# Windowed attention into a mixture-of-depths layer: half-block probability operands, sums closed one unit later, and stores on another queue

## The chip, the core and the metric

The kernel runs on one core of a Trainium2 chip. A core has a matrix engine (TensorE, PE in the profile; its weight loads are listed as PEld), a vector engine (VectorE, DVE), an engine for activation functions (ScalarE, ACT), a general one (GpSimd, POOL) and SyncE (SP), which here only starts transfers. Each engine works through its own list of instructions in order; semaphores order work between engines. Matmuls write to PSUM, a small accumulator memory; the other data lie in SBUF. DMA engines carry data between the chip's main memory and SBUF; a transfer is started by an instruction on SyncE's or on GpSimd's queue. The metric is the time in microseconds on the device. The hardware profiler records one execution; its span, from the first to the last instruction, is a little shorter than the time.

## The reference

There are 4 batches of 8 heads, 768 positions and head size 64. Attention lets a query see the 128 latest positions up to its own, and the first 4 positions (the sinks). A second stage picks, in each batch, the 128 rows with the largest gate score and adds a gated two-layer network to them.

```
scores = scale * q @ k^T
keep   = (key < 4) | (0 <= query - key < 128)
a      = softmax(where(keep, scores, -1e9))
x      = a @ v                      # heads side by side: (4, 768, 512)
score  = x @ w_gate
top    = the 128 rows of largest score in each batch
out    = x;  out[top] += sigmoid(score[top]) * relu(x[top] @ w1) @ w2
```

## The kernel before

**Tiling.** A batch is cut into six blocks of 128 positions. With keys of block `kc` on the partitions, the queries that see them lie in blocks `kc` and `kc + 1`: 256 columns, or four squares of 64 for each half block of keys. In a square the mask leaves everything, a triangle, or nothing. For the first key half the squares are diagonal triangle, full, opposite triangle, empty; for the second they are empty, diagonal, full, opposite. Heads are handled in two groups `g` of four.

**Scores.** `scores(st, kc, g)` writes two PSUM tiles `sc`, one for each parity of head, by 64 x 64 tiles of the array (L279), adds the masks by matmuls of an identity with mask tiles (L290), and takes exp on ACT into `pt` (L296), which is f32: [128 keys, 4 heads, 256 queries]. Masked squares become zeros.

**Sums.** `pv_sinks(st, j, g)` starts the PSUM tile `xg` of query block `j` with the sink terms (L316, for j >= 2). `pv(st, j, g)` adds the products of probabilities and values (L326) for key blocks `j - 1` and `j`, each with all 128 keys, so that one of its two half blocks of queries meets a square of zeros in each. The values `vbuf` have a column of ones, so that the softmax denominators come out as a 65th column. Then DVE normalizes: L332 takes the reciprocal and L335 multiplies into `x`. `xg` has three PSUM buffers.

**After a block.** `finish_block` stores `x` to `out` (L340, on GpSimd's queue; in batch 0 the stores are held back and issued three at a time in the first two units of batch 1) and, in the last batch, also to `x_last` on SyncE's queue (L346), casts `x` to bf16 on ACT there (L349), and takes the gate scores by a reducing DVE instruction into `junk` and `scol` (L351). `compare` spreads the scores of a block over the partitions by a TensorE transpose (L358) and an ACT copy (L359) and counts larger ones on DVE (L362), for the ranking. `moe_steps` makes the selection of the batch before: a matrix `E`, the row index `idx` (L399) and an indirect gather `xe` from `out` on GpSimd's queue (L406). `mlp_steps` is the two-layer network of batches 0 to 2, run in batch 3 and in the tail; its result is added to `out` by an indirect store (L438). `moe_last` does the same for batch 3 in the tail, with a gather from `x_last` (L504) and a last indirect store (L530).

**Order.** The order on every engine is written out by hand. `unit(b, j, gs)` is one step: sinks of block `j`, scores of block `j + 1`, loads, sums of block `j`, then transposes of the next batch's queries and keys (L251, with copies L255 on DVE and L257 on ACT and four sink columns `ksk` by GpSimd, L259), pieces of the selection and of the network, the comparison of block `j - 1`, and the end of block `j`. Batch 0 takes the head groups one after the other; batches 1 to 3 take both in a unit.

**Loads.** The next batch's values go over SyncE's queue (L92), its keys and queries, cast to bf16 on the way, over GpSimd's (L123), a pair of heads at a time; the network's weights too (L232, L235). A load is made to wait for the latest exp (`exps[-1]`), so that it doesn't run ahead. GpSimd's order in a unit is keys, `ksk`, the gather if there is one, the store of `x`, queries.

Of the kernel before, what the change touches and what calls it, by code (L numbers as in the profile page):

```python
# [9 lines left out]
FP32 = mybir.dt.float32  # L10
BF16 = mybir.dt.bfloat16
# [20 lines left out]
def kernel(  # L32
# [22 lines left out]
    xp = ctx.enter_context(tc.tile_pool(name="xp", bufs=11))  # L55
# [31 lines left out]
    def wait_for(ins, other):  # L87
        tc.add_manual_dep(ins.ins, other.ins.name, mybir.DependencyInfo(
            mybir.DependencyClass.Sync, mybir.DependencyReason.DATA), reason="pace of the loads")
# [12 lines left out]
    def new_state(b):  # L102
        st = BatchState()
        st.b = b
        st.kq, st.pt, st.cm, st.x, st.kf, st.qf, st.xg = {}, {}, {}, {}, {}, {}, {}
        st.v = vbuf[b % 2]
        st.vsk = vsk[b % 2]
        st.ksk = ksk[b % 2]
        return st
# [45 lines left out]
    trif = xp.tile([128, 3, 64], FP32, name="trif", tag="x")  # L155
    nc.vector.memset(trif[:, :, :], 0.0)
    nc.vector.memset(trif[:, 1, :], MASK_NEG)
# [6 lines left out]
    for e in range(2):  # L164
        rows = trif[64 * e:64 * e + 64]
        nc.gpsimd.affine_select(out=rows[:, 2, :], in_=rows[:, 2, :], compare_op=ALU.is_ge,
                                fill=MASK_NEG, base=0, pattern=[[1, 64]], channel_multiplier=-1)
        nc.gpsimd.affine_select(out=rows[:, 0, :], in_=rows[:, 0, :], compare_op=ALU.is_ge,
                                fill=MASK_NEG, base=-1, pattern=[[-1, 64]], channel_multiplier=1)
    msk = cp.tile([128, 2, 3, 64], BF16, name="msk", tag="msk")  # L170
    nc.vector.tensor_copy(out=msk[:, :, :, :], in_=trif[:, :, :].unsqueeze(1).to_broadcast((128, 2, 3, 64)))
    for e in range(2):
        nc.vector.memset(trif[64 * e:64 * e + NSINK, :, :], 0.0)
    msk0 = cp.tile([128, 2, 3, 64], BF16, name="msk0", tag="msk0")
    nc.vector.tensor_copy(out=msk0[:, :, :, :], in_=trif[:, :, :].unsqueeze(1).to_broadcast((128, 2, 3, 64)))
# [90 lines left out]

    exps = []

    def scores(st, kc, g):
        nq = 256 if kc + 1 < NB else 128  # L270
        pt = st.pt[kc, g] = pp.tile([128, 4, 256], FP32, name="pt", tag="pt")
        sc = [ps.tile([128, 2, 256], FP32, name="sc", tag="ps") for _ in range(2)]
        for hh in range(2):
            hp = 2 * g + hh
            for kh in range(2):
                k0 = kc * 128 + 64 * kh
                q0, q1 = (64, nq) if kh else (0, nq if kc == 0 else min(nq, 192))
                for e in range(2):
                    nc.tensor.matmul(  # L279
                        out=sc[e][es[kh], hh, q0:q1], lhsT=st.KT[es[e], hp, k0:k0 + 64],  # L280
                        rhs=st.QT[es[e], hp, kc * 128 + q0:kc * 128 + q1],
                        start=(hh == 0), stop=False, skip_group_check=True)
        sq = [((2, 4), (0, 2)), ((0, 1), (3, 4))] if nq == 256 else [((0, 1), (0, 2))]
        for r, pair in enumerate(sq):
            for kh in range(2):
                s0, s1 = pair[kh]
                m0 = 2 if (s0, s1) == (0, 1) else 1 if s0 == 0 else 0
                m = msk0 if kc == 0 and kh == 0 else msk
                for e in range(2):
                    nc.tensor.matmul(  # L290
                        out=sc[e][es[kh], :, 64 * s0:64 * s1].rearrange("p h (s n) -> p h s n", n=64),
                        lhsT=ident_b[es[e], es[e]], rhs=m[es[e], :, m0:m0 + s1 - s0, :],
                        start=False, stop=(r == len(sq) - 1), skip_group_check=True)
        po = pt[:, :, :].rearrange("p (a e) n -> p e a n", e=2)
        for e in range(2):
            exps.append(nc.scalar.activation(out=po[:, e, :, 0:nq], in_=sc[e][:, :, 0:nq], func=ACT.Exp,  # L296
                                             scale=0.125))
# [11 lines left out]

    def pv_sinks(st, j, gs):  # L310
        for g in gs:
            st.xg[g] = x_ps.tile([128, 4, VS], FP32, name="xg", tag="xg")
        for m in range(2 if j >= 2 else 0):
            q0 = (j - 2) * 128 + 64 * m
            for g in gs:
                nc.tensor.matmul(out=st.xg[g][es[m], :, :], lhsT=st.psk[es[g], q0:q0 + 64],  # L316
                                 rhs=st.vsk[es[g], :, :], start=True, stop=False, skip_group_check=True)

    def pv(st, j, g):
        xg = st.xg[g]  # L320
        terms = [(j, 0)] if j == 0 else [(j - 1, 128), (j, 0)]
        for hh in range(4):
            h = 4 * g + hh
            for kc, off in terms:
                for m in range(2):
                    nc.tensor.matmul(out=xg[es[m], hh, :],  # L326
                                     lhsT=st.pt[kc, g][:, hh, off + 64 * m:off + 64 * m + 64],
                                     rhs=st.v[:, kc, h, :],
                                     start=(j < 2 and hh == 0 and kc == terms[0][0]),
                                     stop=(hh == 3 and kc == j), skip_group_check=True)  # L330
        rz = sp.tile([128, 4, 1], FP32, name="rz", tag="rz")
        nc.vector.reciprocal(out=rz[:, :, :], in_=xg[:, :, D:D + 1])  # L332
        if g == 0:
            st.x[j] = xp.tile([128, DM], FP32, name="x", tag="x")
        nc.vector.tensor_tensor(  # L335
            out=st.x[j][:, 256 * g:256 * g + 256].rearrange("p (h d) -> p h d", h=4),
            in0=xg[:, :, 0:D], in1=rz[:, :, :].to_broadcast((128, 4, D)), op=ALU.mult)

    def store_x(st, j):
        nc.gpsimd.dma_start(out=out[st.b, j * 128:(j + 1) * 128, :], in_=st.x[j][:, :])  # L340

    def finish_block(st, j):
        if st.b:
            store_x(st, j)
        if st.b == B - 1:
            nc.sync.dma_start(out=x_last[j * 128:(j + 1) * 128, :], in_=st.x[j][:, :])  # L346
            if j == 0:
                st.xb = mp.tile([128, NB, DM], BF16, name="xb", tag="xb")
            nc.scalar.copy(out=st.xb[:, j, :], in_=st.x[j][:, :])  # L349
        junk = mp.tile([128, DM], BF16, name="junk", tag="junk")  # L350
        nc.vector.tensor_tensor_reduce(  # L351
            out=junk[:, :], in0=st.x[j][:, :], in1=wgb[:, :], scale=1.0, scalar=0.0,
            op0=ALU.mult, op1=ALU.add, accum_out=st.scol[:, j:j + 1])


    def compare(st, j):
        bc = ps.tile([128, 128], FP32, name="bc", tag="ps")
        nc.tensor.transpose(out=bc[:, :], in_=st.scol[:, j:j + 1].to_broadcast((128, 128)), identity=ident_f[:])  # L358
        nc.scalar.copy(out=st.sbc[:, j * 128:(j + 1) * 128], in_=bc[:, :])  # L359
        n = 128 * (j + 1)  # L360
# [174 lines left out]
    def start_state(st):  # L535
# [12 lines left out]
    qk_loads_0 = {(0, 4): ([(0, 0)], []), (0, 5): ([(0, 1)], []), (1, 0): ([(1, 0)], [(1, 1)]),  # L548
                  (1, 1): ([(2, 0)], [(2, 1)]), (1, 2): ([(3, 0)], [(3, 1)])}
# [4 lines left out]
    def loads(b, j, gs, end):  # L554
        nxt = states.get(b + 1)
        gate = None if end else exps[-1]
# [19 lines left out]

    def unit(b, j, gs):
# [4 lines left out]
        pv_sinks(st, j, gs)  # L582
        if j == 0:
            for g in gs:
                scores(st, 1, g)
                pv(st, 0, g)
            loads(b, j, gs, 0)
            pack_sinks(st, gs)
            sink_scores(st, gs)
        else:  # L590
            if j + 1 < NB:
                for g in gs:
                    scores(st, j + 1, g)
            elif ahead:
                scores(ahead, 0, 0)
            if (b, j) != (B - 1, NB - 1):
                loads(b, j, gs, 0)
            if ahead and j == 5:
                transposes(ahead, 3 if b else 2)
            if b == 0 and gs[0] == 0 and j >= 4:  # L600
                transposes(st, j - 2)
            for g in gs:
                pv(st, j, g)
                if end and g == 0:
                    compare(st, j - 1)
        first = 2 if b else 3
        if ahead and first <= j <= (4 if b else 5):
            transposes(ahead, j - first if j < 5 else 3)
# [4 lines left out]
        if last and not end and (j or b):  # L613
            compare(*((st, j - 1) if j else (states[b - 1], NB - 1)))
        if b and j == 1:
            next(select[b - 1])
        if (b, j) in layers_late:
            next(mlp[layers_late[b, j]], None)
        if last:
            finish_block(st, j)  # L620
        loads(b, j, gs, 1)
        if b == 1 and j < 2:
            for i in range(3 * j, 3 * j + 3):
                store_x(st0, i)
# [65 lines left out]
```

## Time and profile before

| What | Value |
|---|---|
| Time, median of 3 runs | 159.06 us (157.86 to 159.28) |
| Span of the profiled execution | 155.5 us |
| exp, `pt<-sc` 128x512, L296 | 80 times, 616 ns |
| products of probabilities and values, L326 | 1408 records (two for each f32 product), 49.9 us of PE busy |
| sinks, L316 | 128 records, 13.9 us of PE busy |
| scores and masks, L279 and L290 | 384 and 352 records |
| stores of `x`, L340, on GpSimd | 24, 650 ns each, 5.6 us to landing |
| software queue (GpSimd's), hardware queue (SyncE's) | 51.4% and 25.6% of the 16 DMA engines' span |

Busy time counts an engine's own work; a wait is put down to what released it last, and where the named releaser had long been done, the wait was for something else, often a transfer. Pages and timelines give a line as L326, the engine, the operation, what it writes and what it reads (`out<-in`) and its shape; a number in brackets at the end is the idle time of the engine just before, with its releaser. PEclk is the granted TensorE clock in tenths of full speed, and DMA the mean busy share of the 16 DMA engines.

### The profile page before, as it was taken

The numbers are of one execution on the slowest core, as the hardware profiler recorded it, in microseconds if no ns is written. First come the engines' busy times: TensorE is split into PE (matmuls) and PEld (weight loads), VectorE is DVE, ScalarE is ACT, GpSimd is POOL, SyncE is SP. The second block draws the span as 40 slices with busy tenths as digits, with TensorE's granted clock in tenths as the row PEclk, the third lists the DMA queues.
The fourth block names the chain that finished last, engine by engine and source line by source line (L and its number), as shares of the span: only waits on it lengthen the run. The fifth ranks groups of instructions, "written<-read, shape, count | busy, mean of one in ns | idle before, by whom it ended". The sixth has DMA issues, their size and how long they took to land.

```text
span 155.5 us, 6898 instructions
## 1 busy us (share of the span) xinstructions
PE 128.6 (83%) x3014; PEld 99.7 (64%) x3019; DVE 88.6 (57%) x274; ACT 81.4 (52%) x168; POOL 61.9 (40%) x125
## 2 busy tenths in 40 slices
PE   6979998998899696908999897939999999999300
PEld 2446886876768674905968776828698786867000
DVE  6337264679868754431688957557738338572100
ACT  3367537765695472303596575435966773353000
POOL 4275041742329350671217464533530270547020
PEclk9999999999999999675899999999999999999985
DMA  4989357899919999599559999995999447283310
GB/s 164 275 144 163 86 115 117 142 196 205 229 30 205 268 292 275 109 193 201 134 130 193 184 223 170 248 226 124 181 172 233 112 97 245 26 251 46 93 67 0
DMA packets 39424, 25.52 MB, mean 164 GB/s; under 512 B 26465, under 2 KB 36065, under 8 KB 39394
## 3 DMA queue, kind: packets, MB, share of 16 engines
q0 software_dynamic: 12224, 15.60, 51.4%
q1 hardware_dynamic: 27170, 9.47, 25.6%
q8 instruction: 24, 0.39, 1.0%
q14 instruction: 6, 0.05, 0.2%
HBM read 24.15 MB, written 8.91 MB: 213 GB/s over the span
## 4 chain that ended last, share of the span: by engine, by line
DMA 29%; PE 28%; issue 18%; POOL 8%; ACT 7%; DVE 5%; POOLq 1%; ACTq 0%
DMA qb<-in_q_dram 18%; PE xg L326 9%; DMA out_dram<-gye,idx 7%; PE trp L251 5%; ACT pt L296 4%; DMA xe<-out_dram,idx 3%; POOL out_dram L340 3%; PE w L82 3%; PE xg L316 3%; PE sc L279 3%; DVE KT L255 2%; POOL ksk L259 2%; PE sc L290 2%; ACT QT L257 2%; POOL kb L123 1%
## 5 line engine op out<-in xcount | busy, mean ns | idle before, releaser
L296 ACT ACTIVATE pt<-sc 128x512 f32<-128x512 f32 (+1 forms) x96 | 47.0, 579 | 13.6 <-PE sc L290 13.3
L326 PE MATMUL xg<-vbuf,pt 128*64 128x65 f32 x1408 | 49.9, 227 | 1.0 <-ACT pt L296 0.6
L326 PEld LDWEIGHTS xg<-vbuf,pt 128*64 128x64 f32 x1408 | 45.2, 140 | 5.8 <-issue 1.2
L257 ACT COPY QT<-trp 128x768 bf16<-128x768 bf16 x16 | 12.8, 799 | 28.5 <-PE trp L251 28.4
L362 DVE SCALAR_TENSOR_TENSOR cm<-sbc,scol,tie 128x128 bf16<-128x128 f32 (+5 forms) x23 | 15.3, 665 | 15.1 <-ACT sbc L359 15.0
L279 PE MATMUL sc<-QT,KT 64*64 64x192 bf16 (+3 forms) x384 | 21.0, 251 | 2.2 <-issue 0.8
L332 DVE RECIPROCAL rz<-xg 128x4 f32<-128x4 f32 x48 | 8.7, 181 | 23.6 <-PE xg L326 23.5
L335 DVE TENSOR_TENSOR x<-xg,rz 128x256 f32<-128x256 f32 x48 | 20.4, 424 | 1.7
L290 PE MATMUL sc<-msk,ident_b 64*64 64x256 bf16 (+1 forms) x352 | 19.1, 249 | 0.0
L340 POOL DMA_DIRECT2D out_dram<-x x24 | 15.0, 650 | 8.9 <-DVE x L335 6.5
L279 PEld LDWEIGHTS <-KT 64*64 64x64 bf16 x384 | 11.9, 109 | 10.3 <-issue 5.7
L123 POOL DMA_DIRECT2D kb<-in_k_dram x14 | 10.2, 730 | 19.5 <-ACT pt L296 18.9
L255 DVE COPY KT<-trp 128x768 bf16<-128x768 bf16 x16 | 15.2, 951 | 3.4 <-PE trp L251 3.3
L251 PE MATMUL trp<-ident_b,qb 128*64 128x128 bf16 x192 | 9.0, 236 | 9.2 <-DMA qb<-in_q_dram 9.2
L351 DVE CUSTOM_DVE_ANT_0 junk<-x,wgb 128x512 bf16<-128x512 f32 x24 | 16.5, 686 | 0.1
L259 POOL TENSOR_SCALAR_AFFINE_SELECT ksk<-KT 64x4 bf16<-64x4 bf16 x32 | 7.5, 233 | 18.4 <-DVE KT L255 15.8
L316 PE MATMUL xg<-vsk,psk 64*64 64x260 f32 x128 | 13.9, 426 | 0.3 <-DVE rz L332 0.3
L251 PEld LDWEIGHTS <-qb 128*64 128x64 bf16 x192 | 7.0, 121 | 10.0 <-DMA qb<-in_q_dram 10.0
L290 PEld LDWEIGHTS <-ident_b 64*64 64x64 bf16 x352 | 11.7, 110 | 0.0
L251 PE MATMUL trp<-ident_b,kb 128*64 128x128 bf16 x192 | 9.3, 233 | 2.2 <-issue 1.3
L123 POOL DMA_DIRECT2D qb<-in_q_dram x14 | 10.1, 723 | 0.2 <-issue 0.2
L251 PEld LDWEIGHTS <-kb 128*64 128x64 bf16 x192 | 6.7, 117 | 4.9 <-issue 3.1
(113 smaller groups left out, 137.7 us busy)
## 6 DMA issues: line engine op xcount, KB each, us to landing
out_dram<-x POOLq DMA_DIRECT2D x24, 256.0 KB, 5.6
vbuf<-in_v_dram SPq DMA_DIRECT2D x18, 256.0 KB, 6.2
kb<-in_k_dram POOLq DMA_DIRECT2D x14, 192.0 KB, 6.0
qb<-in_q_dram POOLq DMA_DIRECT2D x14, 192.0 KB, 6.2
w_sb<-in_moe_w_dram POOLq DMA_DIRECT2D x8, 256.0 KB, 6.5
vbuf<-in_v_dram SPq DMA_DIRECT2D x12, 128.0 KB, 3.6
x_last<-x SPq DMA_DIRECT2D x6, 256.0 KB, 3.9
kf<-in_k_dram SPq DMA_DIRECT2D x2, 384.0 KB, 4.0
```

What stands on the lines that cost most here:

```text
L123: ins = nc.gpsimd.dma_start(out=ob[:, :, :, :].rearrange(flat), in_=in_)
L251: nc.tensor.transpose(out=trp[es[h], c, :], in_=src[:, h, c, :], identity=ident_b[:])
L255: nc.vector.tensor_copy(out=o, in_=i)
L257: nc.scalar.copy(out=o, in_=i)
L279: nc.tensor.matmul(out=sc[e][es[kh], hh, q0:q1], lhsT=st.KT[es[e], hp, k0:k0 + 64], rhs=st.QT[es[e], hp, kc * 128 + q0:kc * 128 + q1], sta ...
L290: nc.tensor.matmul(out=sc[e][es[kh], :, 64 * s0:64 * s1].rearrange("p h (s n) -> p h s n", n=64), lhsT=ident_b[es[e], es[e]], rhs=m[es[e], ...
L296: exps.append(nc.scalar.activation(out=po[:, e, :, 0:nq], in_=sc[e][:, :, 0:nq], func=ACT.Exp, scale=0.125))
L316: nc.tensor.matmul(out=st.xg[g][es[m], :, :], lhsT=st.psk[es[g], q0:q0 + 64], rhs=st.vsk[es[g], :, :], start=True, stop=False, skip_group_ ...
L326: nc.tensor.matmul(out=xg[es[m], hh, :], lhsT=st.pt[kc, g][:, hh, off + 64 * m:off + 64 * m + 64], rhs=st.v[:, kc, h, :], start=(j < 2 and ...
L335: nc.vector.tensor_tensor(out=st.x[j][:, 256 * g:256 * g + 256].rearrange("p (h d) -> p h d", h=4), in0=xg[:, :, 0:D], in1=rz[:, :, :].to_ ...
L340: nc.gpsimd.dma_start(out=out[st.b, j * 128:(j + 1) * 128, :], in_=st.x[j][:, :])
L351: nc.vector.tensor_tensor_reduce(out=junk[:, :], in0=st.x[j][:, :], in1=wgb[:, :], scale=1.0, scalar=0.0, op0=ALU.mult, op1=ALU.add, accum ...
```

## The change

There are four parts.

1. **Stores.** `x` is stored over SyncE's queue as soon as it is there, in batch 0 as well. GpSimd issues no plain stores any more. The loads of batch 1's keys and queries are spread over eight units from (0, 2) on. A load at the end of a unit now waits for the unit's last product (`late[0]`).
2. **Scores.** For key blocks 2 to 4 the empty squares are dropped from the layout: a head takes 192 columns, and the second key half is shifted by 64, so that 448 columns are written and exponentiated instead of 512. The mask of both triangles of a half is one matmul for each array tile.
3. **Half-block operands.** For query blocks from the third on, `pv` multiplies with all 128 keys only for the two squares where both halves count; `pv_halves` multiplies the other two squares with 64 keys each, on 64 x 64 tiles of the array, ahead of `pv`.
4. **Sums closed a unit later.** The sinks, the normalization and all that follows from it move to the front of the next unit (`close`); of `compare`, the part on PE and ACT becomes `spread`, and the part on DVE is done a unit later. Halves and sinks write one PSUM region from different rows of the array, so `fence` puts a small DVE memset between them. The last unit has an order of its own, with the sinks between the two groups' products and the halves at the end.

The diff, cut to its core:

```diff
     def scores(st, kc, g):
-        nq = 256 if kc + 1 < NB else 128
-        pt = st.pt[kc, g] = pp.tile([128, 4, 256], FP32, name="pt", tag="pt")
+        w, k0 = width(kc), kc * 128
+        pt = st.pt[kc, g] = pp.tile([128, 2, 512], FP32, name="pt", tag="pt")
...
+                if w == 192:
+                    q0, q1 = (64 * hh, 256) if kh else (0, 192 + 64 * hh)
...
+        elif w == 192:
+            marks = [(kh, slice(0, 2), slice(0, 3, 2)) for kh in range(2)]
...
         for e in range(2):
-            exps.append(nc.scalar.activation(out=po[:, e, :, 0:nq], in_=sc[e][:, :, 0:nq], func=ACT.Exp,
-                                             scale=0.125))
+            exps.append(nc.scalar.activation(out=pt[:, e, 0:n], in_=sc[e][:, 0:n], func=ACT.Exp, scale=0.125))
...
+    def fence(st, j, gs, ins, i, n):
+        if i == 0 and (j, gs) in st.fence:
+            wait_for(ins, st.fence[j, gs])
+        elif i == n - 1 and (j, gs) not in st.fence:
+            mark = sp.tile([1, 1], FP32, name="mark", tag="mark")
+            st.fence[j, gs] = nc.vector.memset(mark[:, :], 0.0)
+            wait_for(st.fence[j, gs], ins)
...
+    def pv_halves(st, j, gs):
+        for g in gs:
+            for hh in range(4):
+                for m in range(2):
+                    f = first(st, j, g, m)
+                    ins = nc.tensor.matmul(out=st.xg[j, g][es[m], hh, :],
+                                           lhsT=prob(st, j - m, g, hh, es[m], 3 * m),
+                                           rhs=st.v[es[m], j - m, 4 * g + hh, :], **f)
+                    fence(st, j, gs, ins, 8 * gs.index(g) + 2 * hh + m, 8 * len(gs))
...
     def pv(st, j, g):
-        terms = [(j, 0)] if j == 0 else [(j - 1, 128), (j, 0)]
+        terms = {0: [(0, 0), (0, 1)], 1: [(0, 2), (0, 3), (1, 0), (1, 1)]}.get(j, [(j - 1, 2), (j, 1)])
...
     def finish_block(st, j):
-        if st.b:
-            store_x(st, j)
+        nc.sync.dma_start(out=out[st.b, j * 128:(j + 1) * 128, :], in_=st.x[j][:, :])
...
-    qk_loads_0 = {(0, 4): ([(0, 0)], []), (0, 5): ([(0, 1)], []), (1, 0): ([(1, 0)], [(1, 1)]),
-                  (1, 1): ([(2, 0)], [(2, 1)]), (1, 2): ([(3, 0)], [(3, 1)])}
+    qk_loads_0 = {(i // 6, i % 6): ([((i - 2) // 2, i % 2)], []) for i in range(2, 10)}
...
-        gate = None if end else exps[-1]
+        gate = late[0] if end else exps[-1]
...
+    def close():
+        for st, j, gs in left:
+            pv_sinks(st, j, gs)
+            for g in gs:
+                normalize(st, j, g)
+        for st, j in ranks:
+            compare(st, j)
...
     def unit(b, j, gs):
...
-        pv_sinks(st, j, gs)
+        close()
...
+        elif end:
+            pv(st, j, 0)
+            pv_sinks(st, j, gs)
+            pv(st, j, 1)
+            spread(st, j - 1)
+            compare(st, j - 1)
+            pv_halves(st, j, gs)
+            cast_x(st, j - 1)
+            for g in gs:
+                normalize(st, j, g)
+            cast_x(st, j)
         else:
...
+            if j >= 2:
+                pv_halves(st, j, gs)
+                left.append((st, j, gs))
             for g in gs:
+                if g == gs[-1] and ahead and j == 5:
+                    transposes(ahead, 3)
...
                 pv(st, j, g)
+                if j == 1:
+                    normalize(st, 1, g)
-        first = 2 if b else 3
-        if ahead and first <= j <= (4 if b else 5):
-            transposes(ahead, j - first if j < 5 else 3)
+        if ahead and 2 <= j <= 4:
+            transposes(ahead, j - 2)
...
-        if b == 1 and j < 2:
-            for i in range(3 * j, 3 * j + 3):
-                store_x(st0, i)
```

## The prediction

> **What bounds the kernel now.** First the page's summary, slices and clock: it shows where TensorE is not full.
>
> ```profile
> span 155.5 us, 6898 instructions
> PE 128.6 (83%) x3014; PEld 99.7 (64%) x3019; DVE 88.6 (57%) x274; ACT 81.4 (52%) x168; POOL 61.9 (40%) x125
> PE   6979998998899696908999897939999999999300
> PEclk9999999999999999675899999999999999999985
> DMA  4989357899919999599559999995999447283310
> ```
>
> PE is full in most slices, so it paces the attention. The hole is at slices 16 to 19 (62 to 78 us), where the clock falls too. Next the table by stretch, cut at the batches (columns: PE, PEld, DVE, ACT, POOL busy with instruction counts, clock, DMA share, GB/s): batches 0 to 3, then the stretch after the last sums.
>
> ```profile
> 10.25:41.00 30.75, 29.41 (x740) 22.55 (x739) 19.17 (x57) 19.31 (x39) 11.77 (x29) 1.00 0.91 155
> 41.00:77.20 36.20, 27.99 (x705) 23.11 (x704) 20.58 (x60) 17.46 (x38) 16.35 (x32) 0.86 0.87 190
> 77.20:106.50 29.30, 25.05 (x710) 20.66 (x706) 20.37 (x61) 16.99 (x37) 12.98 (x25) 1.00 0.98 196
> 106.50:131.90 25.40, 25.05 (x602) 20.11 (x604) 16.00 (x55) 17.69 (x40) 8.51 (x11) 1.00 0.72 164
> 135.00:155.50 20.50, 9.90 (x131) 7.15 (x132) 5.61 (x21) 4.16 (x8) 5.77 (x8) 0.87 0.38 91
> ```
>
> PE is idle 8.2 us in batch 1 and 4.2 in batch 2, hardly at all in 0 and 3. The waits and PE's timeline name the reason; of the five waits of L251 for `qb`, the ones in batch 1 are 1.38, 1.03 and 4.64 us (7.05 in all), in batch 2 0.59 and 1.58, besides 0.92 of "issue".
>
> ```profile
> PE trp L251 <- DMA qb<-in_q_dram: 9.2, 5, 4.6
> 65.57 0.50 PE L251 MATMUL trp<-ident_b,kb 128*64 128x128 bf16 x12
> 70.71 0.85 PE L251 MATMUL trp<-ident_b,qb 128*64 128x128 bf16 x12 [4.64 <-DMA qb<-in_q_dram]
> ```
>
> Last, GpSimd's timeline and the landing times of the stores issued in 50 to 57 us say why that `qb` was late.
>
> ```profile
> 54.31 0.54 POOL L340 DMA_DIRECT2D out_dram<-x  x1 [2.22 <-DMA qb<-in_q_dram]
> 55.06 0.54 POOL L340 DMA_DIRECT2D out_dram<-x  x1 [0.21 <-issue]
> 56.10 0.72 POOL L123 DMA_DIRECT2D kb<-in_k_dram  x1 [0.49 <-ACT sbc L359]
> 56.87 0.42 POOL L259 TENSOR_SCALAR_AFFINE_SELECT ksk<-KT 64x4 bf16<-64x4 bf16 x2
> 63.37 1.04 POOL L406 DMA_INDIRECT xe<-out_dram,idx  x1 [6.08 <-DVE scol L351]
> 64.41 0.58 POOL L340 DMA_DIRECT2D out_dram<-x  x1
> 64.98 0.73 POOL L123 DMA_DIRECT2D qb<-in_q_dram  x1
> DMA to landing us min/median/max: 7.4/8.3/9.6
> ```
>
> The gather `xe` of batch 0 reads `out`, so it needs batch 0's stores, six of which are held back into batch 1. The last goes out at 55.06; with the median landing of 8.3 it is there at 63.4, and the gather starts at 63.37. Its index was ready at 55.2 (L399 ran at 55.02), and `scol`, the name given, is nothing the gather reads: it is a DMA wait under another name. Behind it in GpSimd's order stands the `qb` that PE needs: issued 64.98, landed 70.7.
>
> [...]mean clock 0.51 at 61.5 to 65.0 and 0.50 at 70.7 to 75.2. [...]So moved stores leave DMA work nearly as it is; what is saved is order and GpSimd's time.
>
> **The change part by part.**
>
> *Stores to SyncE, none held back.* 24 issues, 15.0 us busy by row L340, leave GpSimd, and with them its waits for `x`. Batch 0's stores now end early in the first unit of batch 1, two units (some 8 us) before its gather, so the 6.08 us block goes. On SyncE the `v` loads queue behind a store; they are for the next batch, with a batch of slack, so this costs nothing. Of the 7.05 us of `qb` waits in batch 1 I leave 1.5, since DMA is busy there (share 0.87): -5.5. The clock: half speed over 3.5 us (61.5 to 65.0) and 4.5 us (70.7 to 75.2), PE full in both, costs (3.5 + 4.5)/2 = 4.0; [...]I take back 3.7. **Batch 1: -9.2.** In batch 2 the `qb` issues no longer follow a store's 0.58 us issue and 256 KB in the same queue, and the last pair's transposes come later in their unit: of 0.59 + 1.58 + 0.92 = 3.09 us I take **-1.8**.
>
> *Scores of blocks 2 to 4.* The diagonal squares are masked in 4 matmuls instead of 8. Per array tile: before 192 + 192 score columns and 256 + 128 mask columns, 768; after 192 + 256 and 256, 704. Eight 192-column matmuls on four tiles take 0.17 us (85.32 to 85.49), two a tile, so 0.43 ns a column. 64 x 0.43 = 27 ns, times 3 blocks x 2 groups x 4 batches = 24: **-0.65**. The exp goes from 512 to 448 columns; rows of 616 ns (512) and 389 ns (256) give 0.89 ns a column, 57 ns each, 48 times: 2.7 us of ACT, beside PE, so nothing on the path.
>
> *Half-block operands.* For blocks 2 to 5 (4 x 2 groups x 4 batches = 32 times) the 16 products of 128 rows become 8 of 128 rows and 8 of 64. The 16 take 1.08 us (16.23 to 17.31, where 32 records are 16 f32 products), so 8 save 0.54. The 8 halves sit on two diagonal tiles, four on each; no row shows such a product. Four sinks of 260 columns on four tiles take 0.49 us (84.83 to 85.32), 1.88 ns a column, 122 ns for 65 columns: 0.49 if the two tiles overlap, 0.98 if not. [...]I take 0.50, since the scores overlap across tiles: -0.04 x 32 = **-1.3** (bounds -2.9 and +14).
>
> *Sums closed a unit later.* The sinks move from the front of their unit to the front of the next, and with them normalization, store, `junk` and comparison. Same instructions, plus one DVE memset a unit: bounded by the shortest row, a 0.15 us DVE instruction, and by 0.3 with its two hand-overs. It stands behind the halves and is needed a unit later, and what queues behind it on DVE are the `KT` copies, which wait for PE work issued after the halves: nothing. With three `xg` buffers the second group's halves wait for the first group's normalization (0.18 + 0.42 us by L332 and L335); scores (0.77, 85.32 to 86.09) and the first group's halves (0.5) cover it: nothing.
>
> *Tail.* In the last unit nothing covers it. Before, from its first sinks (131.88) to the last `junk` (135.91 + 0.69) are 4.7 us. After, from the previous block's sinks: 0.6, two normalizations 1.2, `junk` and comparison 0.8 + 0.8, the mark, the next comparison 1.1, normalizations 1.2, `junk` 0.7, about 6.7 with the hand-overs; 0.6 of that left the unit before. **+1.4** (bounds 0 and 2).
>
> *Batch 0.* Six stores come into it, two of eight k/q loads fewer stand in its second half; DMA share there is 0.91 over the batch. The last `qb` is now issued one unit later and needed in the middle of block 5, about 5 us on against a median landing of 6.2: **+0.7** (0 to 1.5).
>
> Sum: -9.2 - 1.8 - 0.65 - 1.3 + 1.4 + 0.7 = -10.85; 159.06 - 10.85 = **148.2 us**.
>
> **Rivals.**
> *A, DMA takes over.* Batches 1 and 2 hold 36.2 x 0.87 + 29.3 x 0.98 = 60.2 us of DMA time; without batch 0's six stores (0.67 us each: 256 KB at the 42 ns a KB and engine of the `x_last` packets, over 16 engines), 56.2. My forecast gives the two 65.5 - 11 - 1 = 53.5 us, a share of 1.05. Packets overlap, and 1.10 is seen at 65.6 to 70.7, which speaks against; but if 0.98, batch 2's mean, is the most over a whole batch, they take 57.3: +3.8, **152.0**.
> *B, halves do not overlap.* +0.44 instead of -0.04 for each of 32: +14.1 + 1.3 = 15.4, **163.6**, slower than before. For it: no such product is in the trace. Against: scores and sinks overlap on all four tiles.
> *C, the deferred closing makes a new wait.* DVE is 70% busy in batch 2 (20.37 of 29.3). Were PE to wait one normalization (0.6) in each of the 12 late units of batches 1 to 3, it is 7.2: **155.4**. Against: the cover of 1.3 us above.
>
> **How the numbers follow.** Forecast 0.64, A 0.14, C 0.12, B 0.10. Range 145.5 to 156.0: below, halves at 0.45 (-1.6) and tail and batch 0 at no cost (-2.1), not all together; above, A and C. B is left out. Faster by over 1%: forecast, A and half of C, 0.84; C's worse half within 1%, 0.06; B slower, 0.10.
>
> **What would show it.** Right: no long wait of `xe` or of L251 for `qb` in batch 1, the clock full until the tail, batch 1 some 27 us; halves of both groups near 1.0 us; GpSimd without stores; the tail after the last PE products no shorter. Wrong: DMA share near 1 with waits for `qb` in their old places (A), halves near 2 us (B), or PE waiting for L332/L335 at every unit (C).

## The result, and the profile after

The changed kernel takes **149.86 us** (median of 4 runs, 148.54 to 152.28), the kernel before 159.17 us beside it (4 runs, 157.86 to 160.79). The ratio is **0.9413, with a 95% interval of 0.9305 to 0.9522**. The forecast was 148.2 us, 1.7 us too low. (The ratios here leave disturbed, slower executions out, so a ratio need not be the quotient of two medians, and of four kernels below, with the stores at once on GpSimd, held back on SyncE, with fewer loads and with the old last unit, the profile shows such a slower execution.)

The page's summary and slices of the changed kernel, the same lines that were shown of the kernel before:

```profile
span 147.9 us, 6752 instructions
PE 126.7 (86%) x2923; PEld 99.2 (67%) x2923; DVE 89.3 (60%) x294; ACT 78.5 (53%) x168; POOL 47.2 (32%) x103
PE   6879999999899959989997796979995999999800
PEclk9999999999999996999999999999999999999995
DMA  4839799599996999899469999997996364390801
```

The hole of four slices is gone; dents are left, the deepest (the two 5s) at 52 to 55 and at 111 to 115 us, and before the tail the clock falls only once, behind the first of them (to 0.50, from 54.76 to 58.18). PE's busy time fell by only 1.9 us, so most of the gain is idle time taken out, not work.

The table by stretch, cut at the batches again, then the last unit from its first sinks to its last halves, then the rest (columns as before):

```profile
10.70:41.00 30.30, 28.96 (x712) 22.95 (x712) 19.83 (x63) 19.04 (x39) 11.11 (x30) 1.00 1.03 195
41.00:69.30 28.30, 25.64 (x678) 21.94 (x677) 19.81 (x63) 16.15 (x38) 9.18 (x18) 0.94 1.05 211
69.30:98.50 29.20, 24.96 (x682) 20.90 (x681) 20.33 (x66) 16.50 (x38) 9.90 (x21) 1.00 0.96 188
98.50:125.16 26.66, 24.82 (x577) 19.90 (x576) 14.21 (x52) 16.43 (x39) 5.52 (x6) 1.00 0.70 156
125.16:129.65 4.49, 4.13 (x83) 2.87 (x82) 3.57 (x13) 1.98 (x4) 1.57 (x1) 1.00 0.43 104
129.65:147.90 18.25, 10.12 (x136) 7.16 (x133) 5.82 (x20) 4.14 (x8) 4.97 (x6) 0.88 0.38 97
```

| Stretch | Before | After | Change | Forecast |
|---|---|---|---|---|
| start and batch 0 | 41.0 | 41.0 | 0 | +0.2 |
| batch 1 | 36.2 | 28.3 | -7.9 | -9.7 |
| batch 2 | 29.3 | 29.2 | -0.1 | -2.3 |
| batch 3 and last unit | 28.5 | 31.15 | +2.65 | +0.9 |
| rest | 20.5 | 18.25 | -2.25 | 0 |
| span | 155.5 | 147.9 | -7.6 | -10.85 |

The forecast's -1.95 for masks and halves is spread over the four batches. The profiled execution of before took 157.42 us, 1.75 less than the median of before; that is why the spans differ by 7.6 us and the times by 9.3.

Batch 1 gained, batch 2 did not, and its DMA share is now 1.05 and 0.96 where it was 0.87 and 0.98. GpSimd's timeline shows the gather `xe` of batch 0 with nothing to wait for but its turn:

```profile
51.19 0.72 POOL L124 DMA_DIRECT2D kb<-in_k_dram  x1 [2.20 <-ACT pt L310]
52.73 0.41 POOL L259 TENSOR_SCALAR_AFFINE_SELECT ksk<-KT 64x4 bf16<-64x4 bf16 x2 [0.83 <-DVE idx L452]
53.77 1.04 POOL L459 DMA_INDIRECT xe<-out_dram,idx  x1 [0.62 <-POOL ksk L259]
54.80 0.75 POOL L124 DMA_DIRECT2D qb<-in_q_dram  x1
```

Before, 6.08 us stood in front of it; now 0.62, and the `qb` behind it goes out at 54.8 instead of 64.98. PE's timeline, however, has these waits in batches 1 to 3 (all those over 0.5 us that have a DMA or nothing known, "issue", as releaser):

```profile
55.24 0.42 PE L304 MATMUL sc<-msk,ident_b 64*64 64x256 bf16 x3 [1.81 <-issue]
66.23 1.15 PE L362 MATMUL xg<-vbuf,pt 64*64 64x65 f32 x31 [0.71 <-issue]
80.72 0.30 PE L251 MATMUL trp<-ident_b,kb 128*64 128x128 bf16 x4 [0.70 <-issue]
82.28 0.53 PE L251 MATMUL trp<-ident_b,qb 128*64 128x128 bf16 x12 [1.26 <-DMA qb<-in_q_dram]
92.26 0.30 PE L251 MATMUL trp<-ident_b,kb 128*64 128x128 bf16 x3 [1.28 <-issue]
97.94 0.39 PE L375 MATMUL xg<-vbuf,pt 128*64 128x65 f32 x5 [0.85 <-issue]
114.01 0.59 PE L485 MATMUL ye<-w_sb,hT 128*128 128x512 bf16 x2 [1.76 <-DMA w_sb<-in_moe_w_dram]
```

Only one wait for `qb` is left. The waits named "issue" split a group in the middle (31 of 32 halves, 4 of 12 transposes): an operand would be waited for at the front of a group. They are taken up below. The last wait is one for the network's weights in batch 3.

The 2 us at the end come from an instruction that no step of the prediction had. The view of the line where the kernel ends lists GpSimd's closing DRAIN (times: minimum, median, maximum in ns), before and after:

```profile
L685 POOLq DRAIN  x3: 46/103/6862, 147.8 to 155.2; - x3
```

```profile
L763 POOLq DRAIN  x3: 46/97/4910, 142.2 to 147.6; - x3
```

It lasts 6.86 us before and 4.91 after.

### The profile page after: what moved, and what is told of

It is laid out like the page before. It is cut to its first block, busy times and chain, and to the rows that moved or that the text cites. A ratio compares the mean times of both kernels' runs of the same rounds, so it can differ in the third digit from the quotient of the medians.

```text
span 147.9 us, 6752 instructions
## 1 busy us (share of the span) xinstructions
PE 126.7 (86%) x2923; PEld 99.2 (67%) x2923; DVE 89.3 (60%) x294; ACT 78.5 (53%) x168; POOL 47.2 (32%) x103
## 4 chain that ended last, share of the span: by engine, by line
PE 47%; DMA 21%; issue 13%; ACT 9%; POOL 3%; DVE 2%; POOLq 1%; SPq 0%; ACTq 0%
PE xg L375 12%; DMA qb<-in_q_dram 10%; PE xg L362 8%; PE trp L251 6%; DMA w_sb<-in_moe_w_dram 6%; ACT pt L310 6%; PE sc L287 5%; PE xg L347 5%; DMA qf<-in_q_dram 3%; PE sc L304 3%; DMA out_dram<-gye,idx 2%; PE bc L409 2%; ACT QT L257 2%; PE ye L485 2%; PE hps L479 1%
## 5 line engine op out<-in xcount | busy, mean ns | idle before, releaser
L310 ACT ACTIVATE pt<-sc 128x448 f32<-128x448 f32 (+2 forms) x96 | 44.4, 546 | 10.8 <-PE sc L304 10.3
L375 PE MATMUL xg<-vbuf,pt 128*64 128x65 f32 x896 | 34.4, 225 | 1.0 <-issue 0.9
L375 PEld LDWEIGHTS xg<-vbuf,pt 128*64 128x64 f32 x896 | 29.4, 138 | 5.7 <-issue 3.1
L362 PE MATMUL xg<-vbuf,pt 64*64 64x65 f32 x512 | 22.2, 225 | 1.3 <-issue 0.9
L362 PEld LDWEIGHTS xg<-vbuf,pt 64*64 64x64 f32 x512 | 20.1, 140 | 2.1 <-issue 1.1
L304 PE MATMUL sc<-msk,ident_b 64*64 64x256 bf16 (+1 forms) x256 | 18.1, 258 | 1.9 <-issue 1.8
L259 POOL TENSOR_SCALAR_AFFINE_SELECT ksk<-KT 64x4 bf16<-64x4 bf16 x32 | 6.1, 192 | 25.3 <-DVE KT L255 22.2
L347 PE MATMUL xg<-vsk,psk 64*64 64x260 f32 x128 | 13.4, 400 | 0.0
L304 PEld LDWEIGHTS <-ident_b 64*64 64x64 bf16 x256 | 10.1, 108 | 2.1 <-issue 2.1
L251 PE MATMUL trp<-ident_b,qb 128*64 128x128 bf16 x192 | 8.2, 220 | 2.2 <-DMA qb<-in_q_dram 1.7
```

Of the source, the lines that this page charges most:

```text
L251: nc.tensor.transpose(out=trp[es[h], c, :], in_=src[:, h, c, :], identity=ident_b[:])
L304: nc.tensor.matmul(out=sc[e][es[kh], o:o + 2 * w].rearrange("p (h s n) -> p h s n", h=2, n=64)[:, :, sq, :], lhsT=ident_b[es[e], es[e]], r ...
L310: exps.append(nc.scalar.activation(out=pt[:, e, 0:n], in_=sc[e][:, 0:n], func=ACT.Exp, scale=0.125))
L347: ins = nc.tensor.matmul(out=st.xg[j, g][es[m], :, :], lhsT=st.psk[es[g], q0:q0 + 64], rhs=st.vsk[es[g], :, :], **f)
L362: ins = nc.tensor.matmul(out=st.xg[j, g][es[m], hh, :], lhsT=prob(st, j - m, g, hh, es[m], 3 * m), rhs=st.v[es[m], j - m, 4 * g + hh, :], **f)
L375: late[0] = nc.tensor.matmul(out=st.xg[j, g][es[m], hh, :], lhsT=prob(st, kc, g, hh, slice(0, 128), s), rhs=st.v[:, kc, 4 * g + hh, :], **f)
```

## The experiments

All ran beside the kernel before, in three sets: its medians there were 158.47 us (7 runs), 159.57 (7) and 159.58 (12).

**1. The stores alone, whole.** The kernel before, with this and nothing else of the change:

```diff
-        nc.gpsimd.dma_start(out=out[st.b, j * 128:(j + 1) * 128, :], in_=st.x[j][:, :])
+        nc.sync.dma_start(out=out[st.b, j * 128:(j + 1) * 128, :], in_=st.x[j][:, :])
-        if st.b:
-            store_x(st, j)
+        store_x(st, j)
-        if b == 1 and j < 2:
-            for i in range(3 * j, 3 * j + 3):
-                store_x(st0, i)
```

> The kernel before with its stores on SyncE's queue, issued at once in batch 0 as well; nothing else changed. Order theory (the gain is the gather that no longer waits for held-back stores, and the query loads that no longer stand behind it): the gather of batch 0 starts within 1 us of its turn, no wait of L251 for qb over 2 us in batch 1, GpSimd's closing drain 2 us shorter, 149.5 to 152 us. Squares theory (a good part of the gain is TensorE work saved): 154 us or more.

Measured: 149.79 us (149.25 to 151.02), ratio 0.9457 (0.9399 to 0.9515). Run again in the third set: 150.86, ratio 0.9492 (0.9365 to 0.9619), beside the whole change with 149.29, ratio 0.9455 (0.9394 to 0.9516).

> The kernel before with the stores alone moved, again, on the same chip as the changed kernel. If the rest of the change is worth nothing in sum, the two are within 1 us of each other; if half-block operands and masks still pay, the changed kernel is 1.5 us or more faster.

> The changed kernel again, unaltered, for a comparison on one chip with the three others of this group: 149 to 151 us. Its issue waits stand again at instruction counts of 193 in blocks of 256.

**The stores alone give all of the gain**; what the other parts give and cost adds up to nothing that two measurements can tell from zero. GpSimd's timeline of it:

```profile
58.65 1.45 POOL L405 DMA_INDIRECT xe<-out_dram,idx  x1 [0.62 <-POOL ksk L259]
60.09 0.76 POOL L123 DMA_DIRECT2D qb<-in_q_dram  x1
```

The gather follows its index at once here too.

**2. Held back or not, SyncE or GpSimd.** The two halves of that edit, each alone: batch 0's stores at once, still on GpSimd (the last six lines of the diff above), and all stores on SyncE, batch 0's still held back (its first two lines).

> The kernel before with batch 0's stores issued at once, still on GpSimd's queue. Order theory: the block of the gather goes (6 us of GpSimd, 4.6 of TensorE and the clock behind it), while the stores still stand before the query loads and the closing drain keeps its 6.9 us: 152 to 155 us. Queue theory (what counts is the hardware queue): 158 to 160 us.

> The kernel before with all stores on SyncE's queue, batch 0's still held back into the first two units of batch 1. Order theory: the gather still waits for the last held-back store, and the query load behind it is late again, so only the drain's 2 us and a little of the waits come back: 155 to 158 us. Queue theory: 149 to 152 us.

| Stores on | held back | at once |
|---|---|---|
| GpSimd | 158.47 (before) | 156.63 (154.0 to 157.96), ratio 0.978 (0.968 to 0.9879) |
| SyncE | 154.41 (153.44 to 159.18), ratio 0.9717 (0.9658 to 0.9775) | 149.79, ratio 0.9457 |

By the ratios the two alone give 3.5 and 4.5 us of the 158.47, together 8.6 (1.8 and 4.1 by the medians, together 8.7). Within their intervals they add up: what the hold and the queue cost is much alike, and neither alone is the gain. Both times lie between the ranges that the two theories expected, so each theory is right in part. At once on GpSimd, that engine's timeline, then PE's:

```profile
57.83 1.05 POOL L405 DMA_INDIRECT xe<-out_dram,idx  x1 [0.41 <-POOL ksk L259]
58.87 0.61 POOL L340 DMA_DIRECT2D out_dram<-x  x1
59.46 0.73 POOL L123 DMA_DIRECT2D qb<-in_q_dram  x1
```

```profile
67.53 0.53 PE L251 MATMUL trp<-ident_b,qb 128*64 128x128 bf16 x12 [3.26 <-DMA qb<-in_q_dram]
```

The gather is free, but `qb` goes out behind a store in the same queue and PE waits 9.1 us for `qb` in four places. On SyncE but held back, GpSimd's timeline, then PE's:

```profile
63.97 1.05 POOL L406 DMA_INDIRECT xe<-out_dram,idx  x1 [8.80 <-DVE scol L351]
65.00 0.76 POOL L123 DMA_DIRECT2D qb<-in_q_dram  x1
```

```profile
70.57 0.85 PE L251 MATMUL trp<-ident_b,qb 128*64 128x128 bf16 x12 [4.88 <-DMA qb<-in_q_dram]
```

The old block is back in full. The trace is of an execution of 159.18 us, so what this kernel gains can't be read from it. It shows that `qb` no longer follows a store, that PE waits 6.06 us for `qb` where it waited 9.22 before, and that the DRAIN is 4.91 us as after. So the prediction read the block rightly, and what it called "order and GpSimd's time" was worth about as much as the block: the hold costs 3.5 us on GpSimd's queue and 4.1 on SyncE's by the ratios.

**3. The whole change, with its stores on GpSimd.** `nc.sync` back to `nc.gpsimd` in `finish_block`.

> The changed kernel with its stores back on GpSimd's queue, still issued at once. Order theory: the gather is not blocked; 24 issues of 0.65 us return to GpSimd and the closing drain is 6.9 us again, so 2 us for the drain and up to 2 for later query loads: 152 to 154 us. Queue theory: 157 us or more.

Measured: 154.55 us (151.78 to 155.6), by the medians 4.7 above the change. The profiled execution is the fastest, 151.78 us; it is 2.15 above the profiled one of the change, and its DRAIN of 6.86 us accounts for 1.95 of that. Its trace also has 3.7 us of waits for `qb`. With four executions so far apart the size stays open between the two. Across six kernels the DRAIN goes with the 24 stores alone: 6.86, 6.87 and 6.86 with them on GpSimd, 4.91 in each of the three without.

**4. What "issue" is.** If one numbers all records of PE, its weight loads and its sequencer in order of start, the "issue" waits of the changed kernel (over 0.3 us) stand at 1217, 2241, 2753, 3521, 4033 and 4289, give or take one: each at the 192nd to 194th of a block of 256. The kernel before has 1472, 2496, 4032 and 4288, again the 192nd. The page's list of queues names a candidate:

```profile
q8 instruction: 23, 0.38, 1.1%
```

The instruction queue carries 23 packets (0.38 MB, 16 KB each), and 23 blocks of 256 are 5,888, against 5,895 records of PE. My reading, the instruction-fetch theory, is an estimate from these counts: a packet holds 256 of PE's instructions, and where the DMA engines are full (share 1.05 in batch 1) it comes late. Two runs to try it: one shifts the program (64 short products in place of ten wide ones at the start, 108 more PE instructions), one takes DMA traffic away (no value loads for batches 2 and 3, which then multiply with what is in the buffers).

```diff
-    keep_warm(10)
+    for _ in range(64):
+        nc.tensor.matmul(out=wx[:, 0:64], lhsT=warm[:, 0:128], rhs=warm[:, 0:64], start=True, stop=True)
```

```diff
-            load_v(nxt, j, slice(0, H), gate=gate)
+            if nxt.b < 2:
+                load_v(nxt, j, slice(0, H), gate=gate)
```

> The changed kernel with the ten wide warming products at its start replaced by 64 short ones, 108 instructions more on TensorE ahead of everything else. Instruction-fetch theory: the issue waits stay at instruction counts of 193 in blocks of 256, so they stand 108 instructions earlier in the work, between other products than before. Any cause in the work itself (a buffer, a semaphore): they stay between the same products. Time within 1.5 us of the changed kernel either way.

> The changed kernel without the loads of values for batches 2 and 3 (they are left out; these batches use the values of batches 0 and 1), so 3 MB of small packets less on the DMA engines in batches 1 and 2. Instruction-fetch theory (the waits of TensorE called issue are for its instructions[...]): the issue waits over 0.3 us in batches 1 and 2, 5.4 us in the changed kernel, fall under 2, 145.5 to 147.5 us. If they have another cause (PSUM, semaphores): they stay, 149 to 150.5 us.

Shifted: 151.76 us (one run), 1.9 above the change, where at most 1.5 was expected. PE's timeline has the waits in other work:

```profile
52.32 0.53 PE L251 MATMUL trp<-ident_b,kb 128*64 128x128 bf16 x12 [0.98 <-issue]
...
86.03 0.81 PE L362 MATMUL xg<-vbuf,pt 64*64 64x65 f32 x19 [1.59 <-issue]
92.73 0.62 PE L362 MATMUL xg<-vbuf,pt 64*64 64x65 f32 x13 [2.14 <-issue]
```

Their counts are 2240, 2496, 3008, 3776, 4032, 4288 and 4544, still the 192nd of a block, give or take one: **the waits go with the count, not with the work**. With fewer loads: 143.93 us (142.28 to 145.12), ratio 0.895 (0.8847 to 0.9053). Its PE timeline and a row of its table by stretch:

```profile
55.81 0.30 PE L304 MATMUL sc<-msk,ident_b 64*64 64x256 bf16 x3 [0.55 <-issue]
65.20 1.15 PE L362 MATMUL xg<-vbuf,pt 64*64 64x65 f32 x31 [0.51 <-issue]
79.47 0.30 PE L251 MATMUL trp<-ident_b,kb 128*64 128x128 bf16 x4 [0.70 <-issue]
89.36 0.30 PE L251 MATMUL trp<-ident_b,kb 128*64 128x128 bf16 x3 [1.02 <-issue]
```

```profile
41.00:69.30 28.30, 26.69 (x736) 22.53 (x738) 21.04 (x67) 17.35 (x40) 9.72 (x21) 1.00 0.93 179
```

The same places of the program wait, 2.8 us in sum instead of 5.35 (under 2 was expected), `qb` is waited for nowhere in batch 2, and the clock stays full. The smaller sum by itself shows little, since it differs by more between two executions of the changed kernel (below). But twelve loads of 1024 packets at 19.0 ns over 16 engines, 14.6 us of DMA time, were taken out, and batches 1 and 2 became 5.5 us shorter (from batch 1's first `psk` to batch 3's: 57.4 to 51.9). So DMA paces these two batches in the changed kernel.

The packet records of the traces give the times for it; what a packet holds they don't show. In the changed kernel the five waits of batches 1 to 3, each beside the packet of the instruction queue with the number of its block (the eighth, tenth, thirteenth, fifteenth and sixteenth), in us:

| Packet starts | Packet ends | PE goes on | Between |
|---|---|---|---|
| 52.75 | 53.86 | 55.24 | 1.38 |
| 62.56 | 64.85 | 66.23 | 1.38 |
| 78.51 | 79.47 | 80.72 | 1.25 |
| 89.89 | 90.77 | 92.26 | 1.49 |
| 95.56 | 96.51 | 97.94 | 1.43 |

Over the 14 traces of this case there are 84 "issue" waits over 0.2 us at such places (and two elsewhere, of 0.20 and 0.22), and each ends 1.21 to 1.64 us after its block's packet has ended; none of the 230 such places that PE passed without one was reached earlier than 1.21 us after it (in the kernel before and the changed one: 11 waits, 1.25 to 1.5 us after; 34 places without, none earlier than 1.29). A packet starts later where the DMA engines are full: a median of 1.0 us after PE passes the same place of the block before where the DMA share of the next 2 us is under 0.8 (94 places), and 2.7 us where it is over 1.0 (168 places); 0.9 (15) and 2.75 (25) in these two kernels.

The repeat of the changed kernel has no wait for `qb` and 10.5 us of those waits, where the first profile had 5.66, beside 1.7 for `qb`, 1.76 for `w_sb` and 1.7 lost to the clock (10.8 in sum). Both took the same time, 149.6 us. That fits DMA engines that set the pace (share over 41 to 99 us: 1.01 in the first profile, 0.98 in the repeat), whichever piece is late.

**5. Halves and masks undone.** The changed kernel with four squares again for blocks 2 to 4 (512 columns, eight masks), and 128 keys in place of 64 in the products of `pv_halves`:

```diff
-        return 256 if kc < 2 else 192 if kc + 1 < NB else 128
+        return 256 if kc + 1 < NB else 128
...
-                                           lhsT=prob(st, j - m, g, hh, es[m], 3 * m),
-                                           rhs=st.v[es[m], j - m, 4 * g + hh, :], **f)
+                                           lhsT=prob(st, j - m, g, hh, slice(0, 128), 3 * m),
+                                           rhs=st.v[:, j - m, 4 * g + hh, :], **f)
```

> The changed kernel with all four squares again: 512 columns of scores and exp for blocks 2 to 4, and 128-row operands in place of the half-block ones. The stores, the order and the late closing stay. Squares theory (the smaller operands save TensorE time): 151.5 us or more. Order theory: 0.65 us for the masks and at most 0.7 for the rest of the products: 150 to 151.2 us; the exp's 2.7 us of ScalarE don't show.

Measured: 154.98 us (154.07 to 157.06), ratio 0.9695 (0.9608 to 0.9782). PE's timeline of a unit, halves undone, then the changed kernel:

```profile
49.49 1.15 PE L362 MATMUL xg<-vbuf,pt 128*64 128x65 f32 x32
50.48 1.10 PE L375 MATMUL xg<-vbuf,pt 128*64 128x65 f32 x32
```

```profile
49.06 1.10 PE L362 MATMUL xg<-vbuf,pt 64*64 64x65 f32 x32
50.10 1.15 PE L375 MATMUL xg<-vbuf,pt 128*64 128x65 f32 x32
51.08 0.51 PE L251 MATMUL trp<-ident_b,kb 128*64 128x128 bf16 x12
```

Both groups' 16 half products take 1.04 us (49.06 to 50.10) and with 128 keys 0.99; with the 16 others, 2.02 us from 49.06 to 51.08, where they take 1.92 with halves undone (49.49 to 51.41) and took 2.02 and 1.92 before, in two units of batch 1. **Halves save no PE time.** Why this run is 5 us slower is then not their size: its span is 4.45 us longer than the change's, and the trace gives about 2.0 to waits (it has 187 more PE instructions), 1.7 to a second fall of the clock and 0.65 to masks. With one profile, and such waits 5 us apart between two executions of one kernel, that split is open.

**6. When sums are closed.** Three versions of the changed kernel: (a) every unit closes its own sums at its end; (b) the last unit goes as before the change (sinks first, halves, then each group's products and normalization), and the unit before it closes its own sums; (c) both.

```diff
                 pv(st, j, g)
                 if j == 1:
                     normalize(st, 1, g)
+            for s_, j_, g_ in left:
+                pv_sinks(s_, j_, g_)
+                for g in g_:
+                    normalize(s_, j_, g)
+            left.clear()
```

```diff
         elif end:
-            pv(st, j, 0)
             pv_sinks(st, j, gs)
-            pv(st, j, 1)
             spread(st, j - 1)
-            compare(st, j - 1)
-            pv_halves(st, j, gs)
             cast_x(st, j - 1)
-            for g in gs:
-                normalize(st, j, g)
+            pv_halves(st, j, gs)
+            pv(st, j, 0)
+            compare(st, j - 1)
+            normalize(st, j, 0)
+            pv(st, j, 1)
+            normalize(st, j, 1)
```

> The changed kernel with sinks, normalization, store and gate score closed at the end of their own unit again (blocks 2 to 5 but the very last, which keeps its order). Deferral theory (the later closing pays by hiding the vector engine's work): 151 us or more, with TensorE waiting for normalizations. Tail theory (the later closing only lengthens the last unit): the stretch from the last unit's first product to the last gate score is about 1.4 us shorter, 148 to 149.5 us.

> The changed kernel with its last two units closed as in the kernel before: block 4 of the last batch in its own unit, and in the last unit sinks first, then halves, then the two groups, the first normalized while the second is summed. Tail theory: from the last unit's first product to the last gate score 4.7 us or less instead of 6.3, 1 to 1.5 us less than the changed kernel on this chip. If the end is set elsewhere (the scatter-adds of the network): no difference, within 0.5 us.

> The changed kernel with every unit closed at its own end and the last unit as in the group's other variant. If late closing hides nothing, it is as fast as the variant with only the last two units closed early, within 1 us; if it pays in the body, it is 1.5 us or more slower than that.

| Version | Time, us | Ratio |
|---|---|---|
| the change, same set as (b) and (c) | 149.29 (148.6 to 158.06) | 0.9455 (0.9394 to 0.9516) |
| (a) own unit | 151.25 (149.04 to 153.37) | 0.94 (0.9274 to 0.9526) |
| (b) old last unit | **147.86** (145.24 to 150.93) | **0.9261 (0.9183 to 0.9339)** |
| (c) both | 151.21 (149.69 to 152.68) | 0.9564 (0.9477 to 0.9651) |

(a) can't be told from the change. But (b) beats both the change and the kernel before, and (c) against it prices late closing where units follow: 3.35 us by the medians, 4.8 by the ratios, with intervals apart. The four don't give one price, though: the change against (a), the same difference with the block before the last in it, shows none, and (a) against (c), where only the order of the last unit differs, shows no gain from the old order (151.25 and 151.21 us, in two sets). PE's timeline of the last unit, the change and then (b):

```profile
128.56 1.15 PE L362 MATMUL xg<-vbuf,pt 64*64 64x65 f32 x32 [0.36 <-DVE mark L339]
```

```profile
126.00 0.67 PE L347 MATMUL xg<-vsk,psk 64*64 64x260 f32 x8
...
126.87 1.15 PE L362 MATMUL xg<-vbuf,pt 64*64 64x65 f32 x32
127.95 1.15 PE L375 MATMUL xg<-vbuf,pt 128*64 128x65 f32 x32
```

In the change the halves of the last block come last of all and wait for the mark; in (b) they are first, and normalization runs beside products. From the first sinks to the last gate score, the change has 6.3 us (125.16 to 131.46), (b) 4.6 (126.00 to 130.61), before 4.7 (131.88 to 136.60). The change's stretch holds the sinks of the block before, 0.6 us, which the two others have done by then; without them it is 1.0 us longer than before.

## Why the prediction was right, and where it was not

- **The block of the gather: right.** Read from one wait put down to `scol` and a median landing time. The gather now waits 0.62 us, and putting the hold back alone brings an 8.80 us block back. Of -9.7 in batch 1 (with its share of masks and halves), -7.9 came; taking back 3.7 of the clock's 4.0 was too much, as one fall of 3.4 us (54.8 to 58.2) is left and costs 1.7. It follows an "issue" wait of 1.81 us, which I had not seen as possible. That the clock would stay full once the long waits were gone was my estimate. Nor was PE idle all through the time ahead of a fall: in the 3.41 us ahead of this one (51.35 to 54.76) PE was busy for 2.08, and ahead of the first one before (58.12 to 61.53) for 1.93. And the block was not nearly the whole of it: freeing the gather alone gives 3.5 us by the ratio, and the rest took the other queue.
- **"-1.8 in batch 2": this step failed.** It took the waits there as a matter of order in GpSimd's queue. The one wait for `qb` went from 1.58 to 1.26 us and waits of "issue" joined it. Batch 2 had a DMA share of 0.98 before the change and has 0.96 after it, and with fewer loads it got shorter (28.8 to 26.3 us, from `psk` to `psk`), so the DMA engines pace it in the changed kernel. What I gave to rival A was so: batches 1 and 2 take 57.5 us, against 53.5 in the forecast and 57.3 in A. I had used a peak of 1.10 over 5 us to set a share of 1.05 over two batches; 1.05 was held in one, not in both.
- **Why the total still came near.** Two things make up for it: the DRAIN, -1.95, and batch 0, 0 instead of +0.2; and the profile of before, from which the terms came, is of an execution 1.6 us shorter than the 159.06 from which their sum was taken. The DRAIN and the shorter execution were not in the forecast, so the nearness is in part luck: by the spans -7.6 came of -10.85. Rival A had the batches right and, with 152.0, the time further off.
- **The other queue: worth more than GpSimd's issues.** That the DMA work stays nearly as it is, the lists of queues confirm: the two hold 77.0% of 155.5 us before and 81.7% of 147.9 after, 119.7 and 120.8 us. But the same transfers on another queue were worth 5.1 us by the ratios with the stores at once (0.978 and 0.9457), beside a DRAIN 1.95 us shorter and waits for `qb` of 0.35 us (1.41 in the repeat) where there were 9.14.
- **Halves, -1.3: the term was mis-sized.** Eight were taken as 0.50 us and took 0.52; the eight of 128 keys that they replace were taken as 0.54 and take 0.50 (half of 49.49 to 50.48). The two tiles do overlap: otherwise, as in rival B (163.6 us), eight would have taken near 1.0. But by an estimate from these figures the products of 128 keys run two at a time as well: eight in 0.50 us are 62 ns each, where the prediction works out 122 from the sinks for one alone. So half the rows bought nothing here, on two of the four tiles. The 0.45 us of the term's bound (-2.9) was my estimate, and no trace shows it.
- **Scores, -0.65: lost in the time**, since DMA paces (share 1.05 and 0.96 in batches 1 and 2). A group of 12 instead of 16 matmuls takes 0.30 to 0.32 us by the timeline, 0.33 and 0.44 before; but from a unit's first score to its last product it is 2.64 us (48.44 to 51.08) against 2.69 before (49.50 to 52.19), so masks and halves together save 0.05 us a unit, where 0.13 was worked out.
- **Late closing, 0: wrong in its favour, by 3.35 us (medians) or 4.8 (ratios)** where (b) is set against (c), though the change against (a) shows nothing. I looked for a wait it could add (rival C) and not for the wait it takes away: with sums closed in their own unit the sinks and normalization stand at its end, and the next unit's work waits there. In (a) and (c), PE waits 1.9 us for the transposes' copies, 0.7 for the mark and 1.2 for `xe`, of which the change has 0.2, 0.4 and 0. But the "issue" waits are fewer there (2.7 us in each), so what carries the difference stays open.
- **Tail, +1.4: right in kind.** 6.3 us against 4.7, where 6.7 was worked out, so +1.0 by the same sum. Version (b), which restores the old end and closes the block before the last early, gains 1.4 us by the medians and 3.1 by the ratios; that is more than the trace of the last unit accounts for, and the rest is open.
- **Unforeseen:** the 1.76 us wait for `w_sb` in batch 3. Its piece took 9.0 us to land, where the slowest of the same loads took 7.0 before. In the repeat this wait was 0.41, so it moves with the traffic.

## What to carry to other kernels

Ask first which instruction stands behind a waiting one in its queue and who needs that, and follow the wait to the transfer whose landing time fits; here stores held back cost a gather 6 us of waiting, and the hold and the shared queue together cost 8.6 us. Then add up the DMA share of each stage with the forecast's shorter time: if it comes above what a whole stage has ever held (here 0.98 before, 1.05 once after), forecast the DMA time, not the sum of the waits taken out. A reordering that pays inside a loop can cost in the last turn, where nothing follows to hide it: cut the last turn out and give it its own order.

## What was not expected of the hardware

- GpSimd's closing DRAIN took 6.86 us with 24 plain stores issued from GpSimd (before, and 6.87 and 6.86 in two other kernels) and 4.91 with none (the change and two others): 1.95 us, or 0.08 each, an estimate that shares it evenly.
- PE stopped in mid-group at about the 193rd of a block of 256 of its records, for up to 1.81 us in the changed kernel (at a DMA share of 1.05 in that batch) and 2.37 with the stores alone; in sum 5.66 and 10.5 us in two executions of the changed kernel. It went on 1.21 to 1.64 us after a 16 KB packet of the instruction queue had ended. That a program of fewer instructions is worth more than its busy time would be a guess from this; it was not tried.
- The granted clock of the changed kernel was 0.50 for 3.41 us from 54.76, behind a stretch as long in which PE was busy for 2.08 us; before, it fell to 0.50 at 61.53 and 68.36, with PE busy for 1.93 and 1.12 us of the 3.41 ahead. So a wait of 1.81 us with work beside it came with a loss of clock here; in the repeat, with waits of up to 2.15 us, the clock was 1.00 from 41 to 99 us.
- f32 products of 64 keys on two diagonal 64 x 64 tiles took as long in all as those of 128 keys on tiles of 128 x 64: 0.52 and 0.50 us for eight.
